# Retention outputs of a block made in one visit of TensorE instead of two

## The chip, the cores and the metric

The kernel runs on one core of one Trainium2 chip. The metric is the device time of one execution in microseconds; a comparison uses the median of several runs. A profile comes from one profiled execution of its own. Engines are named as in the profile: PE is TensorE's matmuls and PEld its weight loads, DVE is VectorE, ACT is ScalarE, POOL is GpSimd, SP is SyncE, which issues the DMAs here.

## What is computed

The reference is a retention layer followed by a feed-forward layer with the ELU activation, in float32:

```python
batch, n_heads, seq, head_dim = (4, 8, 768, 64)
gamma = 1.0 - 2.0 ** (-5.0 - np.arange(H))
for t in range(S):                       # state: (B, H, 64, 64)
    state = gamma * state + outer(k[:, :, t], v[:, :, t])
    y[:, :, t] = (1 / sqrt(64)) * q[:, :, t] @ state
x = y as (B*S, H*64) = (3072, 512)
h = x @ w_in                             # (512, 2048)
g = where(h > 0, h, exp(min(h, 0)) - 1)
out = g @ w_out                          # (2048, 512)
```

## The kernel before

**Tokens and blocks.** The 3072 tokens are cut into 24 chunks of 128 and six blocks (`tb` 0 to 5) of four chunks, 512 tokens each. A sequence of the batch is 768 tokens long, so its state starts at zero at every sixth chunk.

**Retention of a block.** The recurrence is turned into products over half chunks of 64 tokens. For a block there are five steps, in `retention_step(tb, step)`: step 0 makes the masked scores of both pairs of chunks (`scores`, L312), step 1 the states at each half chunk (`states`, L352), steps 2 to 4 the outputs (`outputs_step`). All their matmuls are 64 x 64 x 64 and lie on a quarter of the PE array each. `outputs(tb, pp)` is a generator for pair `pp`. Its first stage does `within` (L408): 32 matmuls from the masked scores and the values into two PSUM tiles `y`. Its second stage does half of `across` (L423): 16 matmuls from the states; and then two tiny DVE copies into `seen` (L392), which read `y`. Its third stage does the other half of `across`, and two DVE multiplies (L398) by the powers of gamma write the result into `xb`, the input of the feed-forward layer. A matmul whose state is zero is left out. `outputs_step(tb, 0)` runs the first two stages of pair 0, `outputs_step(tb, 1)` those of pair 1, and `outputs_step(tb, 2)` the third stage of both. A float32 matmul is two matmul records and two weight loads in the profile.

**The feed-forward layer.** Both matrix products use Strassen's scheme, with seven products in place of eight, and in most places a second time inside each of the seven ("two-level"). The second product of blocks 1 to 5 is `second_twice`: it runs over seven products `j` in the order `ORDER2 = [1, 2, 6, 7, 5, 3, 4]`, and each is made of seven quarter products `k` in `inner` (L973), each of four matmuls 128 x 128 x 128. Products 3 and 4 of one `j` are made after products 1 and 2 of the next one. Each quarter product uses one weight tile `wq` of 256 KB from a ring of 11 tiles. When it is done, `fetch_small` issues the load of another (L817, L822). DVE makes the sums that the next `j` needs (`ts`, L847; and `next_input`, L787), sums of quarter products (`add`, L985), and ACT copies (L981).

**The order of the work.** The order is written out by hand. The generator `second_twice` yields at named places, and the loop around it calls `retention_step` for the next block at some of them. So TensorE leaves its row of 128 x 128 products for a visit to the 64 x 64 matmuls of the next block and then comes back. `step` counts the yields "first"; a place "end" is the end of a `j` behind its quarter product 5. For block 2, which is prepared during block 1, the list `VISITS` holds all five places. For blocks 3 to 5, which are prepared during blocks 2 to 4, steps 0 and 1 lie in the first product of the layer, and steps 2 to 4 lie at the ends at which `step` is 1, 4 and 5. Block 5 prepares nothing. So there are four rounds, in the profile at about 186 to 228, 266 to 329, 368 to 430 and 468 to 531 us.

The `y` tiles are four of a ring of four PSUM tiles (`ps_r`), which scores, states and two accumulators of the first layer use as well.

Of the kernel before, what the change touches and what calls it, by code (L numbers as in the profile page):

```python
# [18 lines left out]
def kernel(  # L19
# [79 lines left out]
    def load(m, cuts=(0, 2048), behind=None):  # L99

        if m >= NCHUNK:
            return
        t = ldpool.tile([P, 2048], FP32, name="chunk", tag="chunk")
        raw[m] = (
            t[:, 0:1024].rearrange("p (a h c) -> p a h c", a=2, c=C),
            t[:, 1024:2048].rearrange("p (a h d) -> p a h d", a=2, d=D),
        )
        hold(t, behind)
        for lo, hi in itertools.pairwise(cuts):
            nc.sync.dma_start(t[:, lo:hi], qkv[m, :, lo:hi])  # L110
# [169 lines left out]
    def scale_v(m, by_vector=False):  # L280
        if m >= NCHUNK:
            return
        i = chunks[m][1]
        v = raw[m][1][:, 0]
        eng = nc.vector if by_vector or m < 2 else nc.gpsimd
        eng.tensor_tensor(  # L286
            out=v, in0=v, in1=vf[:, i].unsqueeze(2).to_broadcast([C, H, D]), op=ALU.mult
        )
# [28 lines left out]
    def scores(tb, pp):  # L317

        sc = [ps_r.tile([P, 2, HP, D], FP32, name="sc", tag="r") for _ in range(2)]
        for x in range(2):  # L320
            score_products(sc, tb, pp, x)
        for a in range(2):
            nc.vector.tensor_tensor(
                out=raw[tb * CPB + 2 * pp + a][0][:, 1].rearrange("p h c -> p (h c)").rearrange("p (n t) -> p n t", t=D),
                in0=sc[a].rearrange("p x h t -> p (x h) t"),
                in1=cmask.unsqueeze(1).to_broadcast([P, 2 * HP, D]), op=ALU.mult,
            )
# [38 lines left out]
    def states(tb, pp):  # L366

        kvs = [ps_r.tile([P, 2, HP, D], FP32, name="kv", tag="r") for _ in range(2)]
        for x in range(2):
            state_products(kvs, tb, pp, x, range(2))  # L370
        for x in range(2):
            for sub in range(2):
                state_sum(kvs, tb, pp, x, sub)
# [4 lines left out]
    def outputs(tb, pp):  # L378

        y = [ps_r.tile([P, 2 * 2, 2, D], FP32, name="y", tag="r") for _ in range(2)]  # L380
        for x in range(2):
            for j in range(4):
                pt = raw[tb * CPB + 2 * pp + j // 2][0][:, 1].rearrange("p h c -> p (h c)")
                within(tb, pp, x, j, y, lambda p: pt[:, (x * HP + p) * D :][:, 0:D])
        for other in range(2):
            if not other:
                yield
            else:

                for sub in range(2):  # L390
                    seen = epool.tile([P, 8], FP32, name="seen", tag="seen")
                    nc.vector.tensor_copy(seen.rearrange("p (j x) -> p j x", x=2), y[sub][:, :, :, 0])  # L392
                yield
            for x in range(2):
                across(tb, pp, x, other, y)
        i = chunks[tb * CPB + 2 * pp][1]
        for sub in range(2):
            nc.vector.tensor_tensor(  # L398
                out=place_of(x_of(tb)[:, :, 2 * pp * C : 2 * (pp + 1) * C])[:, :, :, sub, :], in0=y[sub],
                in1=place_of(powers[:, :, i * C : (i + 2) * C])[:, :, :, sub, :], op=ALU.mult,  # L400
            )
# [52 lines left out]
    def outputs_step(tb, step):  # L454

        if step == 0:
            held["y"] = [outputs(tb, pp) for pp in range(2)]
        if step < 2:
            next(held["y"][step])
            next(held["y"][step])  # L460
        else:
            for g in held["y"]:
                next(g, None)
# [18 lines left out]
    def flush():  # L482
        while later:
            later.pop(0)()
# [214 lines left out]
    def bank(x):  # L699
        return ps_f.tile([P, 2, TH], FP32, name="p" + x, tag=x, bufs=2 if x == "a" else 1)  # L700

    def kept(ps):
        m = mpool.tile([P, 2, TH], FP32, name="m", tag="m")
        nc.scalar.copy(m, ps)  # L704
        return m
# [217 lines left out]
    def first_rest(n, j, ps):  # L923

        w, x = {
            1: (w_a[n][:, :, 0], xb[:, 0:2, half[0]]), 6: (w_s[n][:, 0], xt[1]), 5: (w_b[n][:, :, 0], xt[0]),
            4: (w_b[n][:, :, 1], xt[3]), 7: (w_s[n][:, 1], xt[2]),
        }[j]
        for fi in range(2):
            for j2 in range(2):  # L930
                nc.tensor.matmul(  # L931
                    ps[:, fi, :], lhsT=w[:, fi, j2, :], rhs=x[:, j2, :],
                    start=(j in (1, 7) and fi == 0 and j2 == 0), stop=(j2 == 1), skip_group_check=True,
                )
# [349 lines left out]
    def retention_step(tb, step):  # L1284
        if tb >= NTB:
            return
        if step == 0:
            scores(tb, 0)
            scores(tb, 1)
        elif step == 1:  # L1290
            states(tb, 0)
            states(tb, 1)
        elif step < 5:
            outputs_step(tb, step - 2)


    tail = iter(())
# [50 lines left out]
    for _ in tail:  # L1348
        pass
    flush()  # L1350
    step, VISITS = 0, [(0, "end"), (2, "middle"), (3, "first"), (4, "end"), (5, "end")]
    for s in sec:
        if s == "first":
            step += 1
# [8 lines left out]
    for tb in range(2, NTB):  # L1363
        more = tb + 1 < NTB
        qa, qd, u2, end = {}, {}, {}, None

        def rest(n, j):
            if j == 1:
                qa[n] = ps_r.tile([P, 2, TH], FP32, name="qa", tag="r") if n == 0 else bank("a")
            if j == 7:  # L1370
                qd[n] = ps_r.tile([P, 2, TH], FP32, name="qd", tag="r") if n == 3 else bank("bd"[n % 2])
            first_rest(n, j, qa[n] if j in (1, 6, 5) else qd[n])

        def bring(n):
            if more:
                load((tb + 1) * CPB + n)
                scale_v((tb + 1) * CPB + n)

        def pop(count=1):
            for _ in range(count):  # L1380
                if later:
                    later.pop(0)()

        bring(0)
        rest(0, 1)
        for _ in tail:
            pass
        tail, parts = iter(()), combine_x_parts()
        for at, j in enumerate(TWICE):
            cur = first_twice(tb, j)  # L1390

            next(cur)
            next(tail, None)
            next(parts, None)
            next(cur)
            for _ in tail:
                pass
            next(parts, None)
            if at == 1:

                first_end(0, "C11", qa[0])()
                bring(1)
            next(cur)
            tail = cur
        next(tail)
        bring(2)

        sec = second_twice(tb, combine_x_twice if more else lambda: None)
        for n in range(NQ):

            rest(n, 6)
            u2[n] = kept(qa[n])
            if n == 0:
                for _ in tail:
                    pass
            if end:
                end()
            pop()
            rest(n, 7)
            m7 = kept(qd[n])  # L1420
            pop(2)
            if n == 2 and more:
                retention_step(tb + 1, 1)
            if n == 3:
                next(sec)
            rest(n, 5)
            end = first_end(n, "C12", qa[n])
            other = first_end(n, "C22", qa[n], m7)
            if n < 3:
                end()  # L1430
                other()
                rest(n + 1, 1)
                first_end(n + 1, "C11", qa[n + 1])()
                rest(n, 4)
                end = first_end(n, "C21", qd[n], u2[n])
                pop()
                if n == 0:
                    bring(3)
                elif n == 1 and more:
                    retention_step(tb + 1, 0)  # L1440
        for _ in range(2):
            next(sec)
        end()
        other()
        rest(3, 4)
        end = first_end(3, "C21", qd[3], u2[3])
        next(sec)
        end()
        flush()
        step = 0  # L1450
        for s in sec:

            if s == "first":
                step += 1
            elif s != "middle" and step in (1, 4, 5):
                retention_step(tb + 1, {1: 2, 4: 3, 5: 4}[step])
            if s == ORDER2[-1]:
                break
        tail = sec
# [51 lines left out]
```

## Time and profile before

| what | value |
|---|---|
| three timed runs | 632.18, 632.34, 633.39 us; median 632.34 us |
| span of the profiled execution, first to last instruction | 631.6 us (0.7 us below the median; a time of its own is not listed for it) |
| PE busy | 623.8 us, 99% |
| DVE, ACT, POOL busy | 482.1, 255.3, 22.1 us |
| mean granted TensorE clock | 0.999 |
| DMA | 136.32 MB, 216 GB/s over the span |

The busy rows are times of one execution on one core. The chain of waits lists the work that ended last, from the first to the last instruction; here it is PE for 98%. In its rows a number behind x counts records, two for each float32 matmul. A piece named "issue" is time in which an engine waited for nothing that the profile shows. The position of an instruction in TensorE's stream is counted in the built program: four instructions for each float32 matmul (two weight loads, two matmuls) and one for each semaphore wait that stands alone.

### The profile page before, as it was taken

To read this page: it belongs to the slowest core of one execution; us is meant where nothing else is said; L and a number is where in the kernel's file an instruction comes from. 1 tells how busy PE (TensorE), PEld (TensorE's weight loads), DVE (VectorE), ACT (ScalarE), POOL (GpSimd) and SP (SyncE) were. 2 spreads that over 40 slices of the span, in tenths; PEclk is the share of its full clock that TensorE was granted. 3 is DMA by queue.
4 is the path that set the end of the run, shared out by engine and by line. 5 is a ranking of instruction groups with operands and counts; after the bars stand their busy time and mean duration, and the time that the engine had idled before them with its cause. 6 is when DMAs were issued, how large, how long until landed. Compare 5 with 4: busy or idle time off the path is not lost.

```text
span 631.6 us, 16140 instructions
## 1 busy us (share of the span) xinstructions
PE 623.8 (99%) x6678; PEld 560.5 (89%) x6678; DVE 482.1 (76%) x882; ACT 255.3 (40%) x476; POOL 22.1 (4%) x30
## 2 busy tenths in 40 slices
PE   8999999999999999999999999999999999999997
PEld 6864578888899999888999989999989999988997
DVE  6688789989799665799585589777489877558975
ACT  6798646025541114553112646112465211366311
POOL 1021000000000000200000100000110000000000
PEclk9999999999999999999999999999999999999999
DMA  8698669699288788306888702889810698700794
GB/s 329 260 416 295 186 202 268 196 272 319 113 266 257 234 258 315 141 2 199 257 258 296 278 2 71 268 280 289 317 64 16 220 310 252 207 17 4 239 309 151
DMA packets 75897, 136.32 MB, mean 216 GB/s; under 512 B 6320, under 2 KB 31792, under 8 KB 70832
## 3 DMA queue, kind: packets, MB, share of 16 engines
q1 hardware_dynamic: 75824, 135.29, 64.9%
q8 instruction: 53, 0.87, 0.5%
q14 instruction: 20, 0.16, 0.1%
HBM read 114.03 MB, written 21.23 MB: 214 GB/s over the span
## 4 chain that ended last, share of the span: by engine, by line
PE 98%; DVE 0%; issue 0%; ACT 0%
PE pa L973 20%; PE pa L931 10%; PE pd L973 10%; PE pb L973 5%; PE pa L885 5%; PE pb L931 4%; PE pa L758 4%; PE pa L535 3%; PE qa L931 3%; PE x L625 3%; PE pd L885 2%; PE qd L931 2%; PE pd L931 2%; PE pd L758 2%; PE pa L625 2%; PE kv L352 2%
## 5 line engine op out<-in xcount | busy, mean ns | idle before, releaser
L981 ACT COPY ms<-pa 128x128 f32<-128x128 f32 x104 | 27.6, 265 | 148.2 <-PE pa L973 148.2
L973 PE MATMUL pa<-ts,wq 128*128 128x128 f32 x560 | 74.2, 275 | 0.0
L973 PE MATMUL pd<-ts,wq 128*128 128x128 f32 x552 | 73.5, 276 | 0.0
L973 PEld LDWEIGHTS pa<-ts,wq 128*128 128x128 f32 x560 | 68.5, 192 | 0.4
L973 PEld LDWEIGHTS pd<-ts,wq 128*128 128x128 f32 x552 | 67.1, 192 | 0.6 <-DVE res L985 0.2
L973 PE MATMUL pa<-gC,wq 128*128 128x128 f32 x480 | 64.6, 278 | 0.0
L492 ACT ACTIVATE r<-r 128x512 f32<-128x512 f32 x96 | 60.5, 631 | 3.1
L973 PEld LDWEIGHTS pa<-gC,wq 128*128 128x128 f32 x480 | 59.0, 192 | 1.3
L491 ACT ACTIVATE r<-gC 128x512 f32<-128x512 f32 x64 | 39.9, 624 | 31.9 <-DVE gC L939 31.9
L985 DVE TENSOR_TENSOR res<-pd,ms 128x128 f32<-128x128 f32 x68 | 19.5, 287 | 39.6 <-PE pd L973 38.4
L495 DVE SCALAR_TENSOR_TENSOR gC<-r,gC 128x512 f32<-128x512 f32 x64 | 42.6, 697 | 0.7 <-ACT r L492 0.7
L847 DVE TENSOR_TENSOR ts<-gC,ts 128x512 f32<-128x512 f32 x60 | 41.3, 688 | 1.0
L847 DVE TENSOR_TENSOR ts<-gC 128x512 f32<-128x512 f32 x60 | 41.0, 683 | 0.0
L286 POOL TENSOR_TENSOR chunk<-chunk,vf 128x512 f32<-128x512 f32 x16 | 19.4, 1212 | 429.6 <-DMA chunk<-in_qkv_dram 429.6
L973 PE MATMUL pb<-gC,wq 128*128 128x128 f32 x240 | 31.7, 275 | 0.0
L1006 ACT COPY res<-pa 128x128 f32<-128x128 f32 x34 | 9.0, 265 | 55.1 <-PE pa L973 55.1
L973 PEld LDWEIGHTS pb<-gC,wq 128*128 128x128 f32 x240 | 29.2, 192 | 0.0
L704 ACT COPY m<-pa 128x512 f32<-128x512 f32 x24 | 14.0, 582 | 33.0 <-PE pa L758 18.7
L939 DVE TENSOR_TENSOR gC<-qa,gC 128x512 f32<-128x512 f32 x8 | 5.5, 692 | 25.0 <-PE qa L931 18.3
L931 PE MATMUL pa<-xt,w_s 128*128 128x256 f32 x96 | 23.0, 382 | 0.0
L931 PE MATMUL pa<-xt,w_b 128*128 128x256 f32 x96 | 23.0, 382 | 0.0
L931 PE MATMUL pa<-xb,w_a 128*128 128x256 f32 x96 | 22.7, 379 | 0.0
(262 smaller groups left out, 1247.4 us busy)
## 6 DMA issues: line engine op xcount, KB each, us to landing
wq<-scratch_dram SPq DMA_DIRECT2D x277, 256.0 KB, 4.4
chunk<-in_qkv_dram SPq DMA_DIRECT2D x22, 1024.0 KB, 8.7
wraw<-in_w_dram SPq DMA_DIRECT2D x15, 1024.0 KB, 6.0
out_dram<-res SPq DMA_DIRECT2D x14, 256.0 KB, 4.1
scratch_dram<-gT SPq DMA_DIRECT2D x12, 256.0 KB, 4.3
scratch_dram<-m SPq DMA_DIRECT2D x12, 192.0 KB, 6.1
scratch_dram<-so SPq DMA_DIRECT2D x4, 512.0 KB, 4.7
scratch_dram<-wi SPq DMA_DIRECT2D x2, 1024.0 KB, 6.5
```

Source lines behind the costliest of these rows:

```text
L286: eng.tensor_tensor(out=v, in0=v, in1=vf[:, i].unsqueeze(2).to_broadcast([C, H, D]), op=ALU.mult)
L491: nc.scalar.activation(e, h, AF.Relu, scale=-1.0)
L492: nc.scalar.activation(e, e, AF.Exp, scale=-1.0)
L495: nc.vector.scalar_tensor_tensor(g, e, -1.0, h, ALU.add, ALU.max)
L625: nc.tensor.matmul(X[j][:, d, :], lhsT=w[j][:, d * P : d * P + P], rhs=x[j], start=(n == 0 and d == 0), stop=at_end, skip_group_check=True,)
L758: nc.tensor.matmul(ps[:, fi, :], lhsT=w[:, fi, j2, :], rhs=x[:, j2, :], start=(begin and fi == 0 and j2 == 0), stop=(j2 == 1), skip_group_ ...
L847: sub = lambda o, x, y: nc.vector.tensor_tensor(out=o, in0=x, in1=y, op=ALU.subtract)
L885: nc.tensor.matmul(ps[:, f, :], lhsT=lhs[f], rhs=xs[j][k], start=(begin and f == 0), stop=True, skip_group_check=True,)
L931: nc.tensor.matmul(ps[:, fi, :], lhsT=w[:, fi, j2, :], rhs=x[:, j2, :], start=(j in (1, 7) and fi == 0 and j2 == 0), stop=(j2 == 1), skip_ ...
L973: nc.tensor.matmul(ps, lhsT=w[:, f, :], rhs=ts[j][k][:, f, :], start=(begin and f == 0), stop=(f == 3), skip_group_check=True,)
L981: nc.scalar.copy(m, ps)
L985: nc.vector.tensor_tensor(out=o, in0=x, in1=y, op=ALU.add)
```

## The change

The outputs of pair 0, which had a visit of their own, are made in the visit of pair 1, directly ahead of them. In blocks 3 to 5 the visit at the end where `step` is 1 is dropped, and the one at `step` 4 does both pairs; in block 2 the visit at (3, "first") is dropped and the one at (4, "end") does both. The visit at `step` 5, with the third stage, stays where it was. Three places in the code change:

```diff
         elif step == 1:
             states(tb, 0)
             states(tb, 1)
-        elif step < 5:
-            outputs_step(tb, step - 2)
+        elif step == 2:
+            outputs_step(tb, 0)
+            outputs_step(tb, 1)
+        elif step == 3:
+            outputs_step(tb, 2)
...
-    step, VISITS = 0, [(0, "end"), (2, "middle"), (3, "first"), (4, "end"), (5, "end")]
+    step, VISITS = 0, [(0, "end"), (2, "middle"), (4, "end"), (5, "end")]
...
             if s == "first":
                 step += 1
-            elif s != "middle" and step in (1, 4, 5):
-                retention_step(tb + 1, {1: 2, 4: 3, 5: 4}[step])
+            elif s != "middle" and step in (4, 5):
+                retention_step(tb + 1, step - 2)
```

TensorE's instructions are the same in number and kind. In each of the four rounds 96 matmul records (88 where a state is zero) and as many weight loads move behind 10 quarter products (block 2) or 21 (blocks 3 to 5). Two `seen` copies per round move with them on DVE, so that four stand in a row. ACT, POOL and SP keep their order.

## The prediction

> **What bounds the kernel now.** I read the page's busy shares first, then the chain of waits around the visits that the change moves, then the waits of TensorE, the DMA queues, and the trace's list of DMA packets.
>
> ```profile
> PE 623.8 (99%) x6678; PEld 560.5 (89%) x6678; DVE 482.1 (76%) x882; ACT 255.3 (40%) x476; POOL 22.1 (4%) x30
> ...
> PEclk9999999999999999999999999999999999999999
> ...
> q8 instruction: 53, 0.87, 0.5%
> ```
>
> TensorE is busy for 99% of the span at an undisturbed clock, so whatever lengthens or shortens its own instruction stream moves the end. The last line is easy to pass over: queue 8 carries instructions. It brought 53 packets of 16,384 bytes. TensorE's records are 6,678 matmuls, 6,678 weight loads and 256 others, 13,612 in all, or 257 for each packet. No other engine here comes near such a number, so these packets are TensorE's program, and I take a packet for a block of 256 instructions.
>
> The chain of waits through the second of the four rounds in which a next block's attention is worked in:
>
> ```profile
> 295.87 0.89 PE pa L973 x8
> 296.76 1.09 PE y L408 x64
> 297.85 0.35 PE y L423 x16
> 298.20 1.25 issue
> 299.46 0.34 PE y L423 x4
> 299.79 1.09 PE pa L973 x8
> 300.88 0.89 PE pb L973 x8
> ...
> 318.75 1.09 PE y L408 x64
> 319.84 0.47 PE y L423 x32
> 320.31 1.09 PE pa L973 x8
> 321.40 0.89 PE pb L973 x8
> ```
>
> Three things stand here. A product of the second level (L973, 8 matmul records) takes 0.89 us and a visit of 96 records takes 1.09 + 0.47 us. The first 64 records of a visit take 1.09 us, where the 32 after them take 0.47 us, so 64 in full flow would take 0.94 us: entering costs 0.15 us. The first product after a visit takes 1.09 instead of 0.89 us: leaving costs 0.20 us. And one visit of the eight that this change touches holds a hole of 1.25 us, put down to "issue", that is, to nothing that the profile shows. The waits of TensorE name it as the only large one after the start:
>
> ```profile
> PE y L423 <- issue: 1.3, 1, 1.3
> ```
>
> Now the packets. In this hole the queue-8 packet started at 297.22 us, lasted 0.89 us and ended at 298.11 us. The packet before it had started at 273.76 us. TensorE went on at 299.46 us, 1.35 us after the packet's end. I read the hole as TensorE out of instructions. A visit uses them fast: 64 instructions (32 weight loads, 32 matmuls) per 0.47 us, 136 per us, against 16 per 0.89 us, 18 per us, in the products.
>
> **Where the blocks begin.** In the built program the visit of 296.76 us starts at TensorE instruction 6445. 64 + 18 matmuls, as many weight loads and one more weight load had gone out before the hole, so a block begins at 6445 + 165 = 6610, and others 256 apart from it. The program has 13,630 TensorE instructions before and after the change, so the same positions hold after. Over the whole trace the start of packet n follows the moment at which block n is used up, and its block is needed 256 instructions later: two blocks are held. In slow stretches packets start up to 4.3 us before the boundary is executed, so the sequencer reads ahead. I take 48 instructions for that (from 18 per us and a shortest delay near 1 us), which makes about 304 instructions from the trigger of a fetch to the need for it.
>
> **How long a fetch takes.** Six packets of the four rounds were triggered inside a visit: 2.58, 2.14, 2.57, 3.48, 2.35 and 2.56 us from trigger to start (starts at 209.07, 321.63, 401.71, 422.90, 501.54 and 522.03 us). Median 2.56 us, plus 0.95 us for the packet, plus the 1.35 us above: 4.9 us, from 4.4 to 5.8 us. With the DMA engines idle the shortest delay in the trace is about 1.0 us, so 3.3 us is the floor. In busy slow stretches delays reach 6 to 8 us. The stretch ahead of the moved visit is busy:
>
> ```profile
> 309.00:318.75 9.75, 9.75 (x92) 9.63 (x93) 6.62 (x14) 1.55 (x6) 0.00 (x0) 1.00 0.97 310
> ```
>
> The column before the last is the DMA share: 0.97.
>
> **The change part by part.** No matmul, copy, DMA or semaphore wait of TensorE is added or taken away. Each of four rounds loses one visit, and its 96 records (88 for a pair in which a state is zero) join the visit of the other pair. Per round one entry and one exit go: 0.15 + 0.20 = 0.35 us, four times, 1.4 us. The hole of 1.25 us goes too, since the block at 6610 is then reached amid slow products, 188 instructions ahead of the visit.
>
> What comes instead: a visit of 384 or 368 instructions without a pause, longer than one block. From the built order of the changed kernel:
> - Round 2: the visit starts at 6798; blocks begin at its instructions 68 and 324. The fetch for 324 is triggered at 324 - 304 = 20, inside the visit, and needed 304 / 136 = 2.2 us later. It takes 4.9 us: a hole of 2.6 us (2.2 to 3.6).
> - Round 3: starts at 9134; blocks at 36 and 292. Trigger 12 instructions ahead of the visit: 0.67 + 0.15 + 2.15 = 3.0 us to the need: a hole of 1.9 us (1.4 to 2.9).
> - Round 4: starts at 11470; blocks at 4 and 260. Trigger 44 instructions ahead: 2.44 + 0.15 + 1.91 = 4.5 us. The trigger lies in the busy slow stretch, so I take a delay of 3.0 us, nearer to the visits' rows, because TensorE stops asking for weights once the visit runs: 5.3 us in all, a hole of 0.8 us (0 to 3.8, with a delay up to 6 us).
> - Round 1: starts at 4398; blocks at 164 and 420, the last 36 instructions behind the visit. Trigger at 116: 268 / 136 + 0.2 + 36 / 18 = 4.2 us: a hole of 0.7 us (0.2 to 1.6).
>
> Together 6.0 us (3.8 to 11.9). TensorE has nothing to give this back with, so it goes to the end.
>
> [...]
>
> VectorE: the two small copies per pair (L392, 0.16 us each) move with their pair; in the merged visit four stand in a row. What queues behind them are sums of products that TensorE makes after the visit, so I cost them at nothing; without that cover it is 0.3 us a round. The closer point is behind the second product, where the removed visit gave VectorE 1.6 us:
>
> ```profile
> 496.62 2.49 DVE L787 TENSOR_TENSOR gC<-gT,gC 128x512 f32<-128x512 f32 x4
> 499.02 0.69 DVE L847 TENSOR_TENSOR ts<-gC 128x512 f32<-128x512 f32 x1
> 499.74 0.69 DVE L847 TENSOR_TENSOR ts<-gC,ts 128x512 f32<-128x512 f32 x1
> ```
>
> In this round TensorE would come to the next product at 498.81 instead of 500.37 us. That product's first quarter reads the first half of L787's result (ready near 497.9), its second at 499.7 the rest (ready at 499.11), and the first use of the L847 tiles is at 502.4, ready at 500.4. The least margin is 0.6 us: nothing is paid. If it is short by that much again, it costs 0.6 us in each of three rounds.
>
> SyncE and GpSimd keep their order. Weight tiles (ring of 11) would be wanted 1.6 us earlier. Their least time from landing to use near the moved visit is 2.8, 3.1 and 2.7 us in rounds 2 to 4, so about 1.2 us is left. The last block, which has no visits, runs down to 2.5 us and does not wait. Nothing.
>
> **Sum.** -1.4 - 1.25 + 6.0 = +3.35 us on a span of 631.6 us. The median of the three runs, 632.34 us, lies 0.7 us above that span, which I leave as it is: 635.7 us. With the low terms +1.15 (633.5), with the high ones +9.25 (641.6).
>
> **The rivals.**
> - Fetches are hidden after all, or the hole at 298.20 had another cause. Then only the savings count: -2.65 us, 629.7 us, faster; 630.9 if a hole of 1.25 us stays somewhere. For it: seven of eight visits have no hole, and visits of the scores and states use 256 instructions each without one. Against it: in rounds 2 to 4 those run with idle DMA queues and delays near 1 us, and no other releaser lies in the hole. It decides if a fetch takes under 2.2 us. Chance 0.16.
> - A fetch inside a long visit takes the idle floor, 3.3 us, because the queues drain while TensorE asks for no weights. Holes of 1.1, 0.3, 0 and 0 us: -2.65 + 1.4 = -1.2 us, 631.1 us. Against it: the six rows above are already such visits. Chance 0.09.
> - No holes, but the weights come late: with the first visit gone, DMA at share 0.97 falls behind by more than the 2.7 us of margin. It would have to lose over 1.1 us a round beyond the 1.6; a loss of 1 us in each of rounds 2 to 4 gives 629.7 + 3 = 632.7 us. The last block speaks against it. Chance 0.04.
>
> **How the numbers follow.** The forecast has 0.71. A measurement of this kernel can tell about 0.2%, 1.3 us, from no change. Faster holds the first rival and a little of the second: 0.18. Within 0.2%: the rest of the second, some of the third, the forecast's low edge: 0.10. Slower: 0.72. The range goes from 631.0 (second rival in, first out) to 640.5 us (the high edge cut, since it wants every delay at its longest).
>
> **What would show it.** In the chain after: four visits of some 192 matmul records, 2.9 us of work each, an "issue" piece of 2 to 3.5 us in round 2 after 324 instructions of the visit, a shorter one in round 3 after 292, perhaps one in round 4 after 260 and one just behind the visit of round 1; no such piece near 298; first products after a visit at 1.09 us four times fewer. Packets of queue 8 ending 1.35 us before each resumption. I am wrong if the merged visits run through in 3.0 us.

## The result and the profile after

| | before | after |
|---|---|---|
| median of 5 runs | 632.34 us | 639.58 us |
| lowest, highest | 632.18, 636.57 | 637.01, 640.09 |
| span of the profiled execution | 631.6 us | 636.5 us (its time: 638.24 us) |

The ratio of after to before is 1.009, 95% interval 1.0065 to 1.0114: slower by 4 to 7 us. The predicted 635.7 us was too little by 3.9 us. The measured time lies in the range, 0.9 us below its upper end; the medians differ by 7.2 us, over twice the forecast 3.35 us.

The page and TensorE's waits of the changed kernel:

```profile
PE 623.7 (98%) x6678; PEld 560.6 (88%) x6678; DVE 483.3 (76%) x882; ACT 255.7 (40%) x476; POOL 21.1 (3%) x30
```

```profile
PE y L408 <- issue: 3.3, 3, 1.8
PE y L423 <- issue: 2.3, 1, 2.3
...
PE pa L973 <- issue: 0.6, 1, 0.6
```

TensorE's work is the same to 0.1 us (623.7 and 623.8 us); what has grown is its time without work. Nearly all of that is "issue", and nearly all of the "issue" stands in or just behind the moved visits. The chain of waits of the changed kernel through the four merged visits, in pieces with start, length and records:

```profile
219.20 1.09 PE pa L973 x8
220.28 0.89 PE pb L973 x8
221.18 0.11 PE pa L973
221.29 0.65 issue
```

```profile
319.61 2.35 issue
321.95 0.57 PE y L423 x22
```

```profile
419.50 1.09 PE y L408 x64
420.59 0.47 PE y L423 x32
421.05 0.80 PE y L408 x50
421.85 1.12 issue
```

```profile
522.42 0.56 PE y L408 x34
522.98 1.82 issue
```

The first is behind the visit of round 1 (which ends at 219.20 us), the others are inside those of rounds 2 to 4. Count the instructions to each hole, two for a matmul record. Round 3: 64 + 32 + 50 = 146 records, so 292 instructions; the block boundary was computed at 292. Round 4, whose first 64 + 32 records are as in round 3: 64 + 32 + 34 = 130 records, 260 instructions; boundary at 260. In round 2, 22 of 184 matmul records follow the hole, so 162 were done, 324 instructions; boundary at 324. In round 1 the hole stands 8 + 8 + 1 = 17 records, 34 instructions, behind the visit (boundary computed at 36). The second round's hole of 1.25 us near 298 us is gone.

The prediction also named the packets of queue 8 as a sign. The DMA view of the 1.1 us from 319.4 us on, in the hole of round 2, has this line:

```profile
q8 instruction: 1, 0.02, 5.5%
```

In the trace's list of packets this one starts at 319.49 us and ends at 320.46 us; TensorE resumes 1.49 us later. In rounds 1, 3 and 4 the packet ends 1.40, 1.32 and 1.32 us before TensorE resumes. In the four traces of the next experiments with holes in the rounds, and in both of the kernel before, this distance is 1.21 to 1.59 us for every hole of over 0.7 us.

### The profile page after: what moved, and what is told of

Same layout as the page of the kernel before. It is cut to its first block, busy times and chain, and to the rows that moved or that the text cites. A ratio compares the mean times of both kernels' runs of the same rounds, so it can differ in the third digit from the quotient of the medians.

```text
span 636.5 us, 16148 instructions
## 1 busy us (share of the span) xinstructions
PE 623.7 (98%) x6678; PEld 560.6 (88%) x6678; DVE 483.3 (76%) x882; ACT 255.7 (40%) x476; POOL 21.1 (3%) x30
## 4 chain that ended last, share of the span: by engine, by line
PE 98%; issue 1%; DVE 0%; ACT 0%
PE pa L973 20%; PE pa L931 10%; PE pd L973 10%; PE pb L973 5%; PE pa L885 5%; PE pb L931 4%; PE pa L758 4%; PE pa L535 3%; PE qa L931 3%; PE x L625 3%; PE pd L885 2%; PE qd L931 2%; PE pd L931 2%; PE pd L758 2%; PE pa L625 2%; PE kv L352 2%
## 5 line engine op out<-in xcount | busy, mean ns | idle before, releaser
L495 DVE SCALAR_TENSOR_TENSOR gC<-r,gC 128x512 f32<-128x512 f32 x64 | 44.3, 724 | 0.7 <-ACT r L492 0.7
```

The lines of the kernel that those rows point to most:

```text
L495: nc.vector.scalar_tensor_tensor(g, e, -1.0, h, ALU.add, ALU.max)
```

## The experiments

Theory: TensorE runs out of instructions, because a merged visit uses a block of 256 faster than the next one comes. Rivals: the long visit stalls by itself or on data, or weights come late. Each ratio is to runs of the kernel before on the same chip: 634.28 us (median of 17 runs) beside the first four kernels and 633.04 us (23 runs) beside the last four.

**Shift the blocks by 80 instructions.** 20 score matmuls of block 1 are made twice (the last argument of `score_products` is a count, 16 without it), which moves every later instruction:

```diff
         for x in range(2):
             score_products(sc, tb, pp, x)
+        if (tb, pp) == (1, 1):
+            for n in range(0, 20, 16):
+                score_products(sc, tb, pp, 1, min(16, 20 - n))
```

> The changed kernel with 20 of the score matmuls of block 1 made a second time, in place (the same values): 80 more TensorE instructions ahead of all four rounds, 80 / 136 per us = 0.6 us of work. Theory (a block of 256 instructions comes late): the block boundaries fall at 84, 244, 212 and 180 of the four merged visits instead of 164, 68, 36 and 4, and the next ones 256 later. Round 1 now has its boundary at 340 of 384, triggered inside the visit: a hole of 2.2 to 3.2 us there (0.65 us before). Rounds 2, 3 and 4 (2.35, 1.12 and 1.82 us before) have none over 0.4 us. Holes in all 2.7 instead of 5.9 us, time about 2.6 us under the changed kernel. Rival (the long visit itself stalls, or a wait for data): holes stay in rounds 2 to 4 as they were, round 1 stays small, time 0.6 us over the changed kernel.

Measured: 640.85 us, ratio to before 1.0108 (1.0087 to 1.0129). The chain in rounds 1 and 3 of this kernel, whose lines lie one further down (L409 is `within`, L424 is `across`):

```profile
221.21 0.21 PE y L424 x10
221.42 2.82 issue
```

```profile
428.60 0.21 PE y L409 x10
428.81 1.08 issue
```

Round 1 behaves as the theory said: with the 64 + 32 + 64 records ahead, the hole comes after 170 records, 340 instructions, hole of 2.82 us where 2.2 to 3.2 was expected. Round 4, now with its boundary at 180, has none. Rounds 2 and 3 were expected to have none over 0.4 us and have 1.89 and 1.08 us. But their holes have moved to the new boundaries: round 3 after 64 + 32 + 10 = 106 records, 212 instructions. So the place is right, and the time for a fetch that is triggered ahead of a visit was taken too short: counted back 304 instruction records from the resumption, the two took 7.4 and 8.0 us. There is also a new hole of 1.5 us in the lengthened score visit. Each measured against the kernel before on its own chip, this kernel is 0.7 us under the changed one, where 2.6 us was expected.

**Shift by 192** (48 matmuls in place of 20).

> The changed kernel with 48 score matmuls of block 1 made a second time: 192 more TensorE instructions ahead of the rounds, 1.4 us of work. Theory: boundaries at 228, 132, 100 and 68. Round 1 none; round 2 a hole of about 1.5 us, just behind the visit (at 388 of 368); round 3 about 2.7 us at instruction 356; round 4 about 2.7 us at 324. In all 6.9 us, time about 2.4 us over the changed kernel. Rival (the visit itself): the holes of the changed kernel, 1.4 us over it.

Measured: 645.15 us, ratio 1.0166 (1.0148 to 1.0184). Holes: 1.20 us after 114 records of round 1 (boundary 228), 1.05 us just behind the visit of round 2, and in the last two:

```profile
426.20 0.35 PE y L424 x16
426.55 2.63 issue
```

The row is from round 3: 2.63 us after 176 records, 352 instructions, four from the boundary at 356, and 2.54 us in round 4. Three of the four came out near the computed 1.5, 2.7 and 2.7 us; round 1 is the same miss as before. Further holes of 1.06 us, in the lengthened score visit, and of 0.66 us, at 81 us, had not been expected; the time is 3.6 us over the changed kernel, again each against the kernel before, where 2.4 us was expected. No rival predicts that round 4's hole goes away with 80 instructions and is 2.54 us with 192.

**Move the merged visits to better places.** In `VISITS` (4, "end") becomes (4, "first"), and in the later blocks:

```diff
-            elif s != "middle" and step in (4, 5):
-                retention_step(tb + 1, step - 2)
+            at = (step, s if s in ("first", "middle") else "end")
+            if at in ({2: (3, "middle"), 3: (3, "first"), 4: (2, "end")}.get(tb), (5, "end")):
+                retention_step(tb + 1, 3 if step == 5 else 2)
```

> The changed kernel with each merged visit moved to the place nearest ahead at which a block boundary falls late in the first 256 instructions: 3, 8, 10 and 14 quarter products earlier in rounds 1 to 4, boundaries at 215, 202, 204 and 238 of the visit. Theory: each fetch then has over 4.9 us to its need: no hole over 0.3 us in any round, the four merged visits run through in about 3.0 us; 1.4 us of entries and exits are saved and the hole of the kernel before is not there: 629.7 us where the kernel before has 632.3, and 8 to 10 us under the changed kernel. Rival (the long visit itself stalls): holes of the same size, time as the changed kernel, 637 to 640 us.

Measured: 634.19 us, ratio 1.0004 (0.9989 to 1.0019). Neither theory's number: the loss against the kernel before is gone and the gain has not come. The chain in rounds 2 and 3:

```profile
310.23 2.51 issue
```

```profile
410.97 1.09 PE y L408 x64
412.06 0.47 PE y L423 x32
412.53 0.93 PE y L408 x64
413.46 0.47 PE y L423 x22
```

Rounds 1 and 3 run through, 2.96 us in round 3, as a long visit can. Compared by the same matmul records before and after, TensorE gains 0.35 us in round 1 and 0.36 us in round 3: the price of one entry and one exit, as computed. Rounds 2 and 4 have holes of 2.51 and 0.99 us at their first boundaries, 202 and 238, whose fetch was triggered 5.7 and 3.7 us ahead of the visit (an estimate: 304 instructions ahead of the boundary, 18 per us in the products). So a late boundary in the visit was not enough.

**Take the data off the queues.** `fetch_small` stops loading after 11 tiles; the 20 repeated matmuls are in as well:

```diff
+        if len(fetched) >= RING:
+            small_w.append((name, fetched[next(turns) % RING]))
+            return
         t = ring.tile([P, 4, P], FP32, name="wq", tag="wq")
+        fetched.append(t)
```

> The changed kernel without the loads of second-level weight tiles after the first 11 (the 11 tiles are used over and over, so those products have other weights), and with the 20 repeated matmuls, so that every merged visit has a boundary triggered inside it: at 358, 306, 318 and 330. With loads as before each would be a hole of about 2.6 us, 10.5 us in all. Theory with a fetch that waits behind the data queue: with little on the queue a fetch takes 1.0 + 0.95 + 1.35 = 3.3 us against 2.2 us of visit, four holes of about 1.1 us. If the delay of a fetch has nothing to do with the data's DMAs, four holes of 2 to 2.8 us. If the weights' coming late made the holes, none at all.

Measured: 638.49 us, ratio 1.0064 (1.0050 to 1.0078); holes of 1.32, 1.18, 1.17 and 0.78 us in rounds 1 to 4. The stretch ahead of the visit of round 2 (the column before the last is the DMA share), and the chain in round 3:

```profile
305.00:321.00 16.00, 16.00 (x223) 15.88 (x224) 11.51 (x23) 2.65 (x10) 0.00 (x0) 1.00 0.05 19
```

```profile
422.56 0.93 PE y L409 x63
423.48 1.17 issue
```

With the DMA share at 0.05 instead of 0.97 there is a hole of 1.1 us on average where 1.1 was computed from an idle fetch of 3.3 us. This tells three things apart. Weights that come late are not the cause: none came. The data's DMAs are the larger part of a hole here: with loads, the four holes whose fetch was triggered well inside a visit were 2.35, 2.82, 2.63 and 2.54 us long, 2.6 us on average, against 1.1 us without. And the rest stays at a DMA share of 0.05, since the visit needs the block some 2.2 us after the trigger (an estimate: 304 instructions at 136 per us). (Two holes outside the rounds, of 0.92 us in the lengthened score visit and 0.64 us at 28 us, are not part of this.)

**The kernel before, one visit 4 quarter products later.** (The expectation says 3. The traces have 32 more records ahead of the visit, which is 4, and the boundary moves by 4 x 16 instructions and 4 lone waits, from 165 to 97.)

```diff
-            elif s != "middle" and step in (1, 4, 5):
-                retention_step(tb + 1, {1: 2, 4: 3, 5: 4}[step])
+            at = (step, s if s in ("first", "middle") else "end")
+            if at in ((2, "first") if tb == 2 else (1, "end"), (4, "end"), (5, "end")):
+                retention_step(tb + 1, {1: 2, 2: 2, 4: 3, 5: 4}[step])
```

> The kernel before with one edit: the first output visit of round 2 is made 3 quarter products later. Its block boundary then falls at its instruction 97 instead of 165, so that the fetch is triggered 207 slow instructions (11.5 us) ahead of the visit instead of 139 (7.7 us). Theory: the hole of 1.25 us at 298 us is gone, nothing else changes: time 0.5 to 1.3 us under the kernel before, depending on how often that one has its hole. Rival (the hole came from something in that place of the work, such as a state's wait): the hole moves with the visit or stays, time the same.

**And the kernel before unchanged, for a second trace.**

> The kernel before once more, unchanged, for a second trace. Theory: if there is a hole in an output visit of rounds 1 to 4, it stands at a block boundary: instruction 165 of the first visit of round 2 is the likeliest, since there the fetch has 9.1 us. It may be missing, if this time the queue was shorter. A hole at another place than a boundary would speak against the theory.

The chain through that visit, first moved, then unchanged:

```profile
301.22 1.09 PE y L408 x64
302.31 0.47 PE y L423 x22
```

```profile
298.22 0.35 PE y L423 x16
298.57 2.08 issue
```

Unchanged, the hole stands behind the same 16 records as in the first trace of before, now 2.08 us long. In the one trace with the visit moved it is gone, and that round is 1.48 us shorter than in the first trace. The times show too little of it to be clear: 632.76 us, ratio 0.9992 (0.9979 to 1.0005).

**Before with the shift of 80.**

> The kernel before with 20 score matmuls of block 1 repeated (80 instructions, 0.6 us). Theory: the boundaries of the eight visits move to 252, 148, 85, 68, 53, 20, 21 and 244; at 252 and 244 the visit is over before its boundary. No hole at the first visit of round 2 (boundary 85); in the others at most one, where a fetch triggered in the busy stretch takes over 8 us (148). Rival (a wait for data at that place): the hole in the first visit of round 2 stays.

One run: 636.08 us. No output visit of the four rounds has a hole. The hole has moved to the lengthened score visit of block 1 (1.86 us in the middle of its matmuls), which the expectation had not considered. Here a shift of 80 helped one place and hurt another.

**Merge only where it held.** Rounds 1 and 3 merged at (4, "first") and (3, "first"), round 2 as in the kernel with one visit moved, round 4 as before.

> Round 2 as in the run before (two visits, the first 3 quarter products later), round 4 as in the kernel before, rounds 1 and 3 merged at the places that had no hole in the aligned kernel (boundaries at 215 and 204). Theory: 0.35 us saved in rounds 1 and 3 each and the hole of round 2 avoided: 1.2 to 2.0 us under the kernel before, if the two fetches triggered ahead of the merged visits do not meet a long queue (then a hole of up to 2.5 us in that run). Rival (merging costs by itself): above the kernel before by 1 to 2 us.

Measured: 631.86 us, ratio to before 0.9979 (0.9967 to 0.9991): faster by 0.6 to 2.1 us, the one kernel here whose whole interval lies under 1. In its one trace no hole stands in the four rounds, and rounds 1, 2 and 3 are 0.36, 1.48 and 0.36 us shorter than in the trace of before.

## Why the prediction was right, and where its sizes were off

**Entries and exits, -1.4 us.** Right: 0.35 and 0.36 us in the merged rounds without a hole.

**The hole of before, -1.25 us.** Right that it goes. It is not a constant: 1.25 us in one trace and 2.08 us in another.

**The new holes, +6.0 us.** Right in sum and place: 0.65 + 2.35 + 1.12 + 1.82 = 5.94 us. One by one, 0.7, 2.6, 1.9 and 0.8 us were predicted. The first two are close. In rounds 3 and 4 the fetch was triggered ahead of the visit, and there the time of a fetch scatters. Counted back 304 instruction records (the prediction's estimate of the trigger) from the resumption, it was 4.3 us in round 3 and 6.6 us in round 4, where 4.9 and 5.3 us were assumed; in rounds 1 and 2 it was 4.9 us, as assumed. That the two errors cancel in the sum is luck. The term that was mis-sized is the delay from trigger to packet start: 2.0 us in round 3 (2.56 assumed) and 4.2 us in round 4, in the "busy slow stretch" (3.0 assumed, on the argument that TensorE's asking no more for weights would shorten it). In the kernel with moved visits round 2's fetch took 10.0 us by the same count, round 4's 6.7 us; hence the failed expectations of that experiment. In the kernel before, a first visit of 176 instructions met a fetch of 10.5 us, in its second trace 11.3 us.

The read-ahead of 48 instructions, which the prediction puts down to a rate of 18 per us, follows from its 4.3 us and shortest delay of 1.0 us only at 9 per us: the packets that start over 4 us ahead of their boundary do so amid products of 16 instructions in 1.73 us. With it the fetch time came out right in rounds 1 and 2, but no run tests the figure by itself.

**The cost of a hole, which was taken at its length.** By start of the same records, TensorE loses 0.45, 0.74, 1.08 and 1.78 us in rounds 1 to 4, 4.05 us against the predicted 3.35 us. Setting off the 0.35 us saved in each round, and in round 2 the 1.48 us that the hole of before cost, the four holes cost 0.80, 2.57, 1.43 and 2.13 us: 0.15 to 0.31 us more each than their "issue" pieces. The four together come to 1.0 us more, less the 0.2 us by which the hole of before cost more than its piece; that makes up the 0.7 us.

**The base.** The prediction set the span of 631.6 us beside the median and took 0.7 us as what lies around it. In the runs of the changed kernel the time is 1.7 to 1.9 us above the span, and in the second trace of before 1.87 us (634.67 to 632.8). So the profiled execution of before probably belongs to a run of about 633.4 us, 1.0 us above the median run. A difference reckoned from its trace is then up to 1.0 us too small against the median, if what lengthened that execution was something that the change removes, such as its hole; this is not shown. Besides, 1.0 us of the 4.9 us between the two spans arises before 45 us, 0.75 us of it before 28 us, where both kernels are the same (pieces of "issue" of 0.37 us at 24.6 us and 0.10 us at 28.9 us are part of it). This is scatter: at the first score visit of round 1 the six traces of kernels that are the same up to there lie up to 2.3 us apart, and the first trace of before is the earliest.

**What was missed: the clock.** The prediction took a hole to cost its own length. In some executions it costs more. In the run with the shift of 80, windows of 3.4 us around the hole of round 2 (the last columns are granted clock, DMA share and GB/s), and in the run with 192 those of round 4:

```profile
324.50:327.90 3.40, 1.51 (x98) 1.38 (x94) 1.87 (x6) 0.00 (x0) 0.00 (x0) 1.00 0.56 193
327.90:331.30 3.40, 3.40 (x53) 3.28 (x43) 0.25 (x2) 0.27 (x1) 0.00 (x0) 0.50 0.03 8
```

```profile
529.00:532.40 3.40, 1.70 (x114) 1.56 (x103) 2.04 (x6) 0.00 (x0) 0.00 (x0) 1.00 0.57 202
532.40:535.80 3.40, 2.56 (x47) 2.49 (x48) 0.24 (x2) 0.27 (x1) 0.00 (x0) 1.00 0.03 8
```

In the first, TensorE was busy for 1.51 us of 3.4 us, and for the next 3.4 us the clock was granted at half: about 1.7 us lost, as an estimate. In the second the hole was longer (2.54 us, not 1.89 us), but it fell on two windows with 1.70 and 2.56 us of work, and the clock stayed. The two half-clock stretches of that first run start at 225.5 and 327.9 us, 102.4 us apart, which is 30 times 3.413 us. The clock record of the kernel before is full from 6.08 to 630.71 us, that of the changed kernel from 6.25 to 637.71 us (1.2 us behind its last instruction), 183.0 and 185.0 times the same 3.413 us, and each is at half behind that; the last 3.41 us ahead of these two ends hold 0.69 and 0.00 us of TensorE's work. That the windows lie on a grid of this step is read from these times alone. The runs with 192 and with moved visits have one half-clock stretch each, from 430.0 and from 313.4 us, behind windows with 0.83 and 0.89 us of work in holes of 2.63 and 2.51 us. Laid exactly on the grid, the first window above holds 1.53 us. One of 1.56 us in the kernel before with the shift of 80 (at 59.98 us), and the one of 1.59 us around the hole of round 4 in the changed kernel, which stands below, were followed by a full clock. So in the windows named here, by the profile's busy time, 1.53 us of work and less had half a clock behind them, and 1.56 us and more a full one. In the kernel before and in the changed one the other windows of the grid hold 1.73 us or more, all with a full clock behind them. No run tests the limit by itself.

```profile
521.66:525.07 3.41, 1.59 (x103) 1.45 (x98) 2.14 (x6) 0.00 (x0) 0.00 (x0) 1.00 0.63 221
525.07:528.48 3.41, 3.41 (x85) 3.34 (x74) 0.54 (x3) 0.27 (x1) 0.00 (x0) 1.00 0.08 22
```

So the changed kernel's profiled execution, with 1.59 us of work in that window, kept its clock.

Three of the five runs of the changed kernel have a mean clock of 0.997 and spans of 637.8 to 638.2 us; the other two have 1.000 and 635.2 and 636.5 us. Half a clock over 3.4 us is 0.27% of the span, which is what 0.997 says. That the clock fell at a hole in those three runs is argued from their mean clock alone. The kernel before has 0.999 to 1.000 in all 17 runs beside the first four kernels and in 22 of the 23 beside the last four; the other has 0.996, at 635.86 us, so it lost clock in that run as well.

The 3.9 us between forecast and median then add up as follows. The spans of the two profiled executions differ by 1.5 us more than forecast: 0.7 us in the rounds and 1.0 us in the start-up, less 0.2 us elsewhere. The time lies 1.8 us above the span and not 0.7 us: 1.1 us. And the median run of the changed kernel, which is one of those with a clock of 0.997, is 1.3 us above the profiled one; one half-clock window, 1.7 us by the estimate above, is more than enough for that.

**The rivals.** Hidden fetches: excluded by the holes at computed positions. Idle floor inside a visit: excluded with loads (2.35, 2.82, 2.63 us), true without them (1.1 us). Late weights: excluded, holes of 0.78 to 1.32 us stay when nothing is loaded. VectorE did not show up as a cause, as costed: from 180 us on, TensorE's waits of over 0.04 us name neither VectorE nor another engine or a DMA in any of the ten traces.

**Left open.** What makes one fetch take 10.0 us and another 4.9 us, from trigger to packet end and 1.35 us more, at a like DMA share (0.90 and 0.93 ahead of the merged visits of rounds 2 and 3 in the kernel with moved visits). It is not mere chance: from trigger to packet start these two took 7.6 and 2.4 us there, and the same two blocks took 7.8 and 2.6 us in the trace of the changed kernel. That the queue's state at the trigger enters is argued from the run without loads, where from round 1 on no such delay is over 5.0 us; no run here isolates it.

## What to carry to other kernels

The small matmuls here used up 136 instructions per us against 18 per us for the large ones, and the merged visits of 368 or 384 instructions, some 2.9 us of work each, met holes of 0.65 to 2.35 us at the next block of 256. In the runs here such a hole came where a fetch was triggered inside the visit or a few us ahead of it; two of the four moved visits, with boundaries at 215 and 204, ran through. Before two short visits are joined to save a change of shape (0.35 us here), count the instructions of the joined visit and see where the blocks begin in the built program. A hole with the releaser "issue" in such a stretch, and an instruction packet that ends shortly before work resumes (1.21 to 1.59 us here), is the sign to look for. Where the visit is moved by a few large products, the hole can go or come: with a move of 4 quarter products the hole of 1.25 us was gone, with one of 8 the hole of 2.35 us in round 2 gave way to one of 2.51 us at another boundary.

## What the hardware showed unexpectedly

- A fetch of 256 TensorE instructions took, from the estimated trigger (304 instructions ahead) to use, 3.3 to 3.8 us in the run without weight loads (four holes of 0.78 to 1.32 us) and 4.8 to 5.3 us when triggered inside a visit with loads. When triggered in a busy stretch it took up to 10.0 us in the kernel with moved visits, and 10.5 and 11.3 us in the two traces of the kernel before.
- In the run with the shift of 80 a hole of 1.89 us was followed by half of TensorE's clock for 3.4 us; in the run with 192 one of 2.54 us was not. The windows of 3.4 us on which they fell held 1.51 us of work in the first run, 1.70 and 2.56 us in the second.
- The hole that is put down to instruction fetch scatters from run to run: behind the same records it was 1.25 and 2.08 us long in two executions of the kernel before.
